# 96 very short matmuls on zeros ahead of the warming matmuls of a chunked-attention and attention-experts kernel

## The chip, the cores and the metric

The kernel runs on one core of one Trainium2 chip. The metric is the device time of one execution in microseconds (us); the medians below are over several executions. A core has five engines that run side by side, each with its own list of instructions, which it takes in order: PE (TensorE, the matrix unit), DVE (VectorE), ACT (ScalarE), POOL (GpSimd) and SP (SyncE, which here only starts DMA transfers). They wait for each other by semaphores. A matmul on PE is two instructions: a weight load (LDWEIGHTS, the rows named PEld) and the matmul proper (MATMUL, the rows named PE).

## The reference

Two stages, all in float32. Batch B = 8, heads 8, sequence S = 576, head width 64.

```python
# stage 1: attention inside chunks of 64 rows, for every head
q_c = q.reshape(B, H, nc, 64, D)            # k_c, v_c alike
scores = scale * np.matmul(q_c, k_c.transpose(0, 1, 2, 4, 3))
attn = softmax(scores)
x = np.matmul(attn, v_c)                    # heads put side by side: x is (8, 576, 512)

# stage 2: four attention experts on x, each token takes two of them
logits = x @ w_gate                         # (8, 576, 4), the two largest per token win
for e in range(4):
    q, k, v = x @ wq[e], x @ wk[e], x @ wv[e]            # width 64
    a = softmax(causal(scale * (q @ k.transpose(0, 2, 1))))
    out += gate[e] * (a @ v @ wo[e])
```

## The kernel before

**Stage 1** goes by groups of 128 rows (36 of them, one or two to a unit). For a group SP loads keys, queries and values (`ks`, `qs`, `vs`, 256 KB each; lines 358, 359 and 362; four buffers of each kind). PE makes the scores as 32 small 64x64 matmuls per group (line 471), which go to the four corners of the array in turn; DVE, ACT and POOL do the softmax (lines 481 to 499); the weights are turned, for the first five groups by PE (line 369, called from line 504) and otherwise by a DMA transpose; and PE makes `x` as 32 matmuls per group (line 544).

**Stage 2** goes by the eight batches: queries and keys of the experts (line 588, three passes of a split into a high and a low part), values and gate logits (line 443), scores of two experts at a time (line 685), exponentials (line 708), turning by PE (line 369), the product with the values (line 779) and the projection out (line 807). The weights `wqk`, `wvg` and `wo` are loaded in the first microseconds (line 412) and split by ACT, DVE and POOL (lines 415 and 419).

**The order.** Every step is added to a plan (`add`, line 75) with its engine, an estimated length and what it depends on. At the end `plan.emit` (line 92) runs through the plan on a clock of its own, with orders that are written out by hand for each engine (`ORDER`, line 191), and emits the instructions in that order. For PE it also fills holes: where PE's next step isn't ready on the planner's clock and the time is before `WARM` (25 us), it emits a **warming matmul** (line 841): 128x512 on the tile `warm`, which is all zeros, into the bank that is last in the list of free banks. The line that does so:

```python
if eng == "PE" and now < until:
    fill()
    free_at[eng] = now + pe_time(0.215, 1.0, now)
```

The planner's clock for PE starts at 0.9 us and is moved only by what `emit` itself emits. 47 warming matmuls come out: 11 ahead of the first real matmuls of line 471, the others between the steps of the first 20 us. `warm` is a 128x512 bf16 tile that DVE zeroes at the start (line 319); `banks` are the eight banks of the accumulator memory. `ctx.enter_context(tc.manual_schedule())` (line 840) makes the framework keep the order in which instructions are issued from there on.

Of the kernel before, what the change touches and what calls it, by code (L numbers as in the profile page):

```python
# [281 lines left out]
def chunked_attention_then_attention_experts(ctx: ExitStack, tc: tile.TileContext, qt, kt, vt, wqk, wvg, wo, out):  # L282
    nc = tc.nc
    pe, dve, act, pool = nc.tensor, nc.vector, nc.scalar, nc.gpsimd
# [6 lines left out]
    def tiles(n, shape, name, dt=F32, src=None):  # L291
        return [(src or sb).tile(shape, dt, name=f"{name}{i}") for i in range(n)]

    banks = tiles(8, [128, 512], "bank", src=psum)
# [23 lines left out]
    warm = sb.tile([128, 512], BF16, name="warm")  # L318
# [477 lines left out]
    def project_out(b):  # L796
        bb = b // 2
        y_op[b] = []
        for t in (range(4) if b % 2 == 0 else range(4, 9)):
            bk, y = Slot(banks), Slot(y_p)  # L800

            def f(t=t, bk=bk):
                w = [t_.rearrange("p (k c) -> p k c", k=2) for t_ in W["wo"]]
                n = 0
                for k in range(2):
                    for up, wp in ((uh, w[0]), (ul, w[0]), (uh, w[1])):
                        pe.matmul(bk.t, up[:, k, 128 * t:128 * t + 128], wp[:, k, :], start=(n == 0), stop=(n == 5))  # L807
                        n += 1
            o = add("PE", 1.41, f, deps=u_op[b] + (u_op[b - 1] if t == 4 else []) + w_op["wo"], uses=[bk])
            y_op[b].append(o)  # L810
            if t % 2:
                o = add("ACT", act_t(512), lambda bk=bk, y=y: act.activation(y.t, bk.t, AF.Copy), deps=[o],
                        uses=[bk, y])
            else:
                o = add("DVE", dve_t(512), lambda bk=bk, y=y: dve.tensor_copy(y.t, bk.t), deps=[o], uses=[bk, y])

            def f(t=t, y=y):
                nc.sync.dma_start(out[bb * 2 * S + 128 * t:bb * 2 * S + 128 * t + 128], y.t)
            o = add("SP", 0.36, f, deps=[o], uses=[y])
            transfer("store", 0.6, o, [y])  # L820
# [6 lines left out]
    for b in range(B):  # L827
# [10 lines left out]
            values(b, pair)  # L838
        project_out(b)
    ctx.enter_context(tc.manual_schedule())  # L840
    plan.emit(lambda: banks and pe.matmul(banks[-1], warm[:, 0:128], warm, start=True, stop=True), WARM)  # L841


# [37 lines left out]
```

## Time and profile before

| | |
|---|---|
| Median of 3 executions | 382.74 us (382.62 to 382.85) |
| The profiled execution | 382.36 us |
| Its span, from the first to the last instruction | 380.4 us |
| PE, matmuls | 372.2 us busy, 5213 instructions |
| PE, weight loads | 315.7 us busy, 5215 instructions |
| ACT / DVE / POOL | 302.6 / 268.5 / 245.1 us busy |
| Mean granted clock of TensorE | 1.000 |
| Warming matmuls (line 841) | 13.2 us busy |
| Instruction transfers, queue q8 | 41 packets, 0.67 MB |

How to read the lines. A row of a **timeline** has the start in us from the span's start, the length, the engine, the line of the kernel, the operation, output and inputs by the program's names, the shape, the number of instructions merged into the row, and in brackets the idle time before it with what ended it. The **chain of waits** follows the work that ended last back to its cause; its rows have start, length and work. A row of **windows** has the stretch, its length, then for each engine the busy time and, in brackets, how many instructions lie in the stretch, then the granted clock, the DMA engines' busy share and GB/s; the columns are PE, PEld, DVE, ACT and POOL, or PE and PEld alone. "issue" means that the engine waited for nothing that the profile shows. Matmuls are pipelined and their ends are modelled: the distance between starts is the safer measure. An "x" ahead of a number is a count. Instructions that only wait are not in the counts.

### The profile page before, as it was taken

The numbers are of one execution on the slowest core, as the hardware profiler recorded it, in microseconds if no ns is written. First come the engines' busy times: TensorE is split into PE (matmuls) and PEld (weight loads), VectorE is DVE, ScalarE is ACT, GpSimd is POOL, SyncE is SP. The second block draws the span as 40 slices with busy tenths as digits, with TensorE's granted clock in tenths as the row PEclk, the third lists the DMA queues.
The fourth block names the chain that finished last, engine by engine and source line by source line (L and its number), as shares of the span: only waits on it lengthen the run. The fifth ranks groups of instructions, "written<-read, shape, count | busy, mean of one in ns | idle before, by whom it ended". The sixth has DMA issues, their size and how long they took to land.

```text
span 380.4 us, 13426 instructions
## 1 busy us (share of the span) xinstructions
PE 372.2 (98%) x5213; PEld 315.7 (83%) x5215; DVE 268.5 (71%) x895; ACT 302.6 (80%) x844; POOL 245.1 (64%) x447
## 2 busy tenths in 40 slices
PE   8999999999999999999999999998999999999996
PEld 3598999977888899788779999877898899977664
DVE  3668878589898775668978487597994298467442
ACT  3555699999958998799887579988996579899731
POOL 7552678986885469975864448959387048876600
PEclk9999999999999999999999999999999999999999
DMA  8977785527779493276989473446786101236534
GB/s 269 392 258 236 201 177 169 98 71 146 130 228 246 93 221 83 57 134 91 293 220 271 137 180 72 112 65 214 142 197 87 25 30 30 30 57 84 165 140 165
DMA packets 88479, 57.24 MB, mean 150 GB/s; under 512 B 68960, under 2 KB 68960, under 8 KB 88416
## 3 DMA queue, kind: packets, MB, share of 16 engines
q1 hardware_dynamic: 88272, 56.12, 59.7%
q8 instruction: 41, 0.67, 0.7%
q10 hardware_dynamic: 144, 0.26, 0.3%
q14 instruction: 22, 0.18, 0.2%
HBM read 30.42 MB, written 9.44 MB: 105 GB/s over the span
## 4 chain that ended last, share of the span: by engine, by line
PE 80%; ACT 9%; DVE 3%; POOL 2%; issue 2%; DMA 2%; POOLq 0%; ACTq 0%; DVEq 0%
PE bank L588 22%; PE bank L443 12%; PE bank L807 12%; PE bank L779 9%; PE bank L685 9%; PE bank L544 4%; PE bank L471 4%; PE bank L369 4%; PE bank L841 3%; ACT at L708 3%; DMA wpT<-wp 2%; POOL at L730 1%; ACT aT L754 1%; ACT aT L385 1%; DVE at L696 1%
## 5 line engine op out<-in xcount | busy, mean ns | idle before, releaser
L730 POOL TENSOR_SCALAR at<-at,st,gate 128x448 f32<-128x448 f32 (+4 forms) x160 | 94.9, 607 | 25.1 <-DVE st L721 21.8
L708 ACT ACTIVATE at<-at,st 64x64 f32<-64x64 f32 (+4 forms) x160 | 88.8, 565 | 4.3 <-DVE st L696 4.1
L588 PE MATMUL bank<-xh,wqk_hi 128*128 128x288 f32 x256 | 77.3, 302 | 0.1
L588 PE MATMUL bank<-xl,wqk_hi 128*128 128x288 f32 x256 | 75.4, 295 | 0.0
L588 PE MATMUL bank<-xh,wqk_lo 128*128 128x288 f32 x256 | 75.4, 294 | 0.0
L696 DVE CUSTOM_DVE_ANT_0 at<-bank,mask 128x448 f32<-128x448 f32 (+4 forms) x160 | 59.9, 421 | 8.0 <-PE bank L685 5.7
L499 POOL TENSOR_TENSOR en<-e,mx 128x512 f32<-128x512 f32 x36 | 37.6, 1058 | 38.3 <-DVE mx L490 23.0
L588 PEld LDWEIGHTS bank<-xh,wqk_hi 128*128 128x128 f32 x256 | 48.0, 187 | 2.5 <-issue 1.0
L588 PEld LDWEIGHTS bank<-xl,wqk_hi 128*128 128x128 f32 x256 | 48.0, 188 | 0.5 <-issue 0.3
L588 PEld LDWEIGHTS bank<-xh,wqk_lo 128*128 128x128 f32 x256 | 48.0, 188 | 0.0
L779 PE MATMUL bank<-aT,vv 128*64 128x448 f32 (+4 forms) x384 | 47.0, 393 | 0.4 <-ACT aT L385 0.3
L779 PEld LDWEIGHTS bank<-aT,vv 128*64 128x64 f32 x384 | 25.0, 137 | 22.3 <-issue 13.7
L385 ACT ACTIVATE aT<-wpT 128x1024 uint16<-128x1024 uint16 x32 | 37.7, 1187 | 3.3 <-DMA wpT<-wp 3.2
L754 ACT ACTIVATE aT<-bank 128x128 f32<-128x128 f32 (+1 forms) x160 | 37.2, 331 | 3.3 <-PE bank L369 2.9
L385 ACT ACTIVATE et<-wpT 128x1024 uint16<-128x1024 uint16 x31 | 36.5, 1183 | 3.6 <-DMA wpT<-wp 3.4
L762 DVE STREAM_TRANSPOSE aT<-at 32x96 f32<-32x96 f32 x128 | 34.4, 269 | 5.3 <-PE bank L779 2.4
L443 PE MATMUL bank<-wvg_hi,xh 128*128 128x260 f32 x128 | 37.0, 289 | 0.0
L376 POOL COPY wp<-at 128x1024 uint16<-128x1024 uint16 x32 | 32.5, 1033 | 6.3 <-DMA wpT<-wp 6.1
L443 PE MATMUL bank<-wvg_lo,xh 128*128 128x260 f32 x128 | 36.3, 283 | 0.0
L443 PE MATMUL bank<-wvg_hi,xl 128*128 128x260 f32 x128 | 36.0, 281 | 0.0
L685 PE MATMUL bank<-kh,qh 64*128 64x288 f32 (+4 forms) x192 | 32.3, 326 | 0.6 <-ACT qh L596 0.5
L376 POOL COPY wp<-en 128x1024 uint16<-128x1024 uint16 x31 | 31.6, 1039 | 1.4 <-DMA wpT<-wp 1.1
(104 smaller groups left out, 895.6 us busy)
## 6 DMA issues: line engine op xcount, KB each, us to landing
ks<-in_kt_dram SPq DMA_DIRECT2D x36, 256.0 KB, 4.4
vs<-in_vt_dram SPq DMA_DIRECT2D x36, 256.0 KB, 4.4
out_dram<-y SPq DMA_DIRECT2D x36, 256.0 KB, 2.1
qs<-in_qt_dram SPq DMA_DIRECT2D x35, 256.0 KB, 4.7
at<-in_wqk_dram SPq DMA_DIRECT2D x4, 256.0 KB, 5.5
wpT<-wp SPq DMA_TRANSPOSE x63, 3.8
at<-in_wvg_dram SPq DMA_DIRECT2D x2, 260.0 KB, 5.6
at<-in_wo_dram SPq DMA_DIRECT2D x2, 256.0 KB, 5.9
```

The costliest lines, as they stand in the source:

```text
L376: pool.tensor_copy(p.t[:, :256 * n].rearrange("p (x n) -> p x n", x=2), src().bitcast(U16).rearrange("p (n x) -> p x n", x=2))
L385: act.activation(put().bitcast(U16).rearrange("p j (q x) -> p j q x", x=2), pt.t[:, :256 * n].rearrange("p (x j q) -> p j q x", x=2, j=n), ...
L443: pe.matmul(bk.t[0:rows, :W_VG], xp[:, k, cols], wp[:, k, :], start=(n == 0), stop=(n == 3 * KT - 1))
L499: pool.tensor_tensor(en.t.rearrange("p (s h k) -> p s h k", s=2, h=HP), ev, rv.to_broadcast([128, 2, HP, 64]), op=OP.mult)
L588: pe.matmul(bk.t[:, :288], wp[:, k], xp[:, k, c0:c0 + 288], start=(n == 0), stop=(n == 3 * KT - 1))
L685: pe.matmul(bks[s].t[:rows(i), at:at + c1 - c0], q[own, cs], k[own, c0:c1], start=(x == 0), stop=(x == 2), skip_group_check=True)
L696: dve.tensor_tensor_reduce(out=a.t[:r, A_OFF[i] + c0:A_OFF[i] + c1], in0=bk.t[:r, at:at + w], in1=mask[:r, m0:m0 + w], scale=1.0, scalar=f ...
L708: act.activation(af, af, AF.Exp, scale=-1.0, bias=st.t[:r, 0, i, 0:1], accum_out=st.t[:r, 1, i, 0:1])
L730: pool.tensor_scalar(af, af, st.t[:r, 2, i, 0:1], gt.t[:r, i, e:e + 1], op0=OP.mult, op1=OP.mult)
L754: act.activation(dst, bk.t[:, s0:s0 + 64 * n].rearrange("p (j c) -> p j c", j=n), AF.Copy)
L779: pe.matmul(bk.t[64 * s:64 * s + 64, c0 - h0:h1 - h0], vs.t[:, j, 64 * (2 * pair + s):64 * (2 * pair + s) + 64], ts[s].t[:, 448 * j + c0:4 ...
L807: pe.matmul(bk.t, up[:, k, 128 * t:128 * t + 128], wp[:, k, :], start=(n == 0), stop=(n == 5))
```

## The change

Right before the planner emits anything, 96 matmuls are issued on PE. Each loads 64 columns of the zero tile as weights and streams 16 columns of it, into the first 64 partitions and 16 columns of the last bank. That is 96 weight loads and 96 matmuls, 192 instructions, at the front of PE's list. They read what the warming matmuls read, and write where those write. Nothing else is changed: the plan, its clock and the warming matmuls stay as they are.

```diff
     ctx.enter_context(tc.manual_schedule())
+    for _ in range(96):
+        pe.matmul(banks[-1][0:64, 0:16], warm[:, 0:64], warm[:, 0:16], start=True, stop=True)
     plan.emit(lambda: banks and pe.matmul(banks[-1], warm[:, 0:128], warm, start=True, stop=True), WARM)
```

## The prediction

> **What bounds the kernel now.** I read the head of the page first: the span, the engines' busy shares and the chain that ended last.
>
> ```profile
> span 380.4 us, 13426 instructions
> ...
> PE 372.2 (98%) x5213; PEld 315.7 (83%) x5215; DVE 268.5 (71%) x895; ACT 302.6 (80%) x844; POOL 245.1 (64%) x447
> ...
> PE 80%; ACT 9%; DVE 3%; POOL 2%; issue 2%; DMA 2%; POOLq 0%; ACTq 0%; DVEq 0%
> ```
>
> PE is busy for all but 8.2 us, and it carries four fifths of the chain. A busy matmul row is not a matmul at its peak, so I asked next what PE waits for, in the view of waits for PE alone. These are all its rows (us in total, times, longest):
>
> ```profile
> PE bank L544 <- issue: 1.3, 1, 1.3
> PE bank L841 <- DVE warm L319: 1.2, 1, 1.2
> PE bank L471 <- issue: 0.6, 1, 0.6
> PE bank L685 <- ACT qh L596: 0.5, 1, 0.5
> PE bank L841 <- issue: 0.3, 2, 0.2
> PE bank L779 <- ACT aT L385: 0.3, 1, 0.3
> ```
>
> Only 0.5 + 0.3 us of this is a wait for another engine in mid-kernel. PE takes its instructions in order, so what is put in front of them moves nearly everything behind, to the end: about 0.8 us at most can be swallowed on the way. What counts is by how much the head grows, and what the shift does to the two long "issue" waits. The head, in PE's timeline (start, length, then the work), with one row of SP's timeline and one of the page's DMA issues:
>
> ```profile
> 1.24 4.87 PE L841 MATMUL bank<-warm 128*128 128x512 bf16 x11 [1.24 <-DVE warm L319]
> 6.05 0.69 PE L471 MATMUL bank<-ks,qs 64*64 64x64 f32 x32
> 6.67 0.61 PE L841 MATMUL bank<-warm 128*128 128x512 bf16 x2
> 7.32 0.69 PE L471 MATMUL bank<-ks,qs 64*64 64x64 f32 x32
> 8.17 4.05 PE L841 MATMUL bank<-warm 128*128 128x512 bf16 x18 [0.16 <-issue]
> ```
>
> ```profile
> 1.25 0.91 SPq L358 DMA_DIRECT2D ks<-in_kt_dram  x2
> ```
>
> ```profile
> ks<-in_kt_dram SPq DMA_DIRECT2D x36, 256.0 KB, 4.4
> ```
>
> The first keys are asked for at 1.25 and land, by the page's median, 4.4 us later, at about 5.7; the first real matmuls (L471) start at 6.05. So the 11 warming matmuls ahead of them cover a real wait almost exactly, and some 0.4 us is left under that cover: nothing hides further work put before them. The planner's clock doesn't know of the new matmuls, so it emits all the warming ones as before.
>
> The rows also show the array's rate. 11 warming matmuls take 4.87 us, 18 later ones 4.05: 0.44 us against 0.225. The rate doubles once, near 6.1, after 4.8 us of uninterrupted work. The granted clock in the windows further down reads 1.00 from the start, so this factor isn't read from there.
>
> **First term: 96 tiny matmuls.** Each loads a 128x64 weight and streams 16 columns, at the half rate. No such pair is in the trace. Nearest are the 128x64 loads at the end of an L779 group, each with a 64-column matmul (a window of L779 alone); then the transposes of L369, with 128-column loads (a piece of the chain); then the 64x64 pairs of L471 above, which go to four corners of the array in turn.
>
> ```profile
> 356.63:356.75 0.12, 0.12 (x8) 0.11 (x4) 1.00 0.00 0
> ```
>
> ```profile
> 153.75 1.03 PE bank L369 x28
> ```
>
> The window's PEld count says that 4 loads begin in 0.115 us: 29 ns a pair. L369 gives 37, and L471 (6.67 - 6.05) / 32 = 19. I take the first, which has the same weight shape, doubled for the half rate: 57 ns, 96 x 57 = 5.5 us. The ends are 19 ns, if the tiny pairs are bound by issue alone (1.9 us), and twice 37, if their loads take as long as the transposes' (7.1 us).
>
> Then the warming ones. A warming matmul streams columns all the time, a tiny one 14 ns (16/512 of 440) of its 57. I credit the tiny stretch with that quarter of its 5.5 us, 1.3 us, towards the 4.8 that the doubling needed. The remaining 3.5 us are 8 warming matmuls at 0.44, and the last 3 at 0.225 take 0.7: 4.2 us, where 6.05 - 1.24 = 4.8 were needed before. The head grows by 5.5 + 4.2 - 4.8 = 4.9 us. With no credit it would be 5.5, with full credit 2.9 (first rival).
>
> The Trainium skill ("TensorE: Matmul & The Clock Gate", Part 1, "What's actually happening") has the rate decided in free-running windows of some 3.4 us, so that the next edge after 6.1 would be near 9.5. By that rule the head would grow by 4.5 us. The trace shows one switch only and can't tell this from my count.
>
> Of this, 0.2 comes back. The two warming matmuls from 6.67 need 0.45 and the second L471 starts only at 7.32, held by its data; later these will have landed. The loads that SP holds until PE frees a buffer move along with PE, and whoever waits for L471 (DVE first) moves too; I add nothing for them, since the wait only shifts. Head: +4.7 us.
>
> **Second term: the stalls inside a group.** The two "issue" waits lie inside runs of identical matmuls, where no data is waited for (PE's timeline, and one group of 64 from the chain):
>
> ```profile
> 32.95 1.09 PE L471 MATMUL bank<-ks,qs 64*64 64x64 f32 x58
> 34.65 0.34 PE L471 MATMUL bank<-ks,qs 64*64 64x64 f32 x6 [0.61 <-issue]
> 34.92 0.40 PE L588 MATMUL bank<-xh,wqk_hi 128*128 128x288 f32 x1
> ...
> 262.42 1.46 PE L544 MATMUL bank<-et,vs 64*64 64x64 f32 x87
> 265.19 0.38 PE L544 MATMUL bank<-et,vs 64*64 64x64 f32 x9 [1.31 <-issue]
> 265.50 0.81 PE L779 MATMUL bank<-aT,vv 128*64 128x128 f32 x6
> ```
>
> ```profile
> 41.58 1.09 PE bank L471 x64
> ```
>
> A group of 64 takes 1.09 us, 17 ns each; the first stalled one took 34.92 - 32.95 = 1.97, so 0.9 was lost. The second run needed 96 x 17 ns = 1.6 and took 3.1: 1.5 lost. What is missing there? PE's code comes in pieces, by the page's queue table, and counting PE and PEld between the stalls tells where pieces end:
>
> ```profile
> q8 instruction: 41, 0.67, 0.7%
> ```
>
> ```profile
> 0.00:34.60 34.60, 32.44 (x599) 22.70 (x601) 20.46 (x51) 18.04 (x43) 18.29 (x49) 1.00 0.81 287
> 34.60:111.92 77.32, 77.12 (x1266) 68.04 (x1267) 63.43 (x216) 68.00 (x191) 61.45 (x105) 1.00 0.65 157
> 111.92:265.10 153.18, 151.28 (x2162) 132.76 (x2160) 114.28 (x385) 131.16 (x360) 104.73 (x187) 1.00 0.68 156
> ```
>
> PE and PEld have 10,428 instructions for 41 pieces: 254 to a piece (PE's own wait instructions, which the views leave out, come on top). Between the stalls lie 2533 + 4322 = 6855 instructions, 27 times 253.9. It is a whole number of pieces, so both stalls sit at a piece's end: where a piece is run through faster than the next can be fetched, PE stands still. With 192 more instructions in front, every end falls 192 instructions earlier in the old order, into other work. In the next fence stand the two old pieces that end in a stall, one as short that doesn't, and then the three shortest pieces of the new cutting, found by counting back (the next has 4.4 us):
>
> ```profile
> 31.09:33.82 2.73, 2.73 (x129) 2.57 (x128) 2.13 (x4) 2.51 (x9) 0.00 (x0) 1.00 0.36 102
> 261.79:263.66 1.87, 1.87 (x142) 1.87 (x135) 1.87 (x10) 1.74 (x7) 1.87 (x3) 1.00 0.42 153
> 197.59:199.88 2.29, 2.29 (x129) 2.19 (x129) 2.29 (x5) 1.78 (x4) 0.00 (x0) 1.00 0.92 287
> 129.74:131.92 2.18, 2.18 (x131) 2.09 (x129) 0.55 (x3) 2.18 (x6) 0.00 (x0) 1.00 0.03 8
> 178.42:180.69 2.27, 2.27 (x129) 2.20 (x132) 1.47 (x9) 2.16 (x7) 1.14 (x2) 1.00 0.95 190
> 219.61:222.16 2.55, 2.55 (x128) 2.39 (x130) 1.43 (x5) 1.16 (x5) 1.72 (x4) 1.00 0.02 5
> ```
>
> The stalled pieces lasted 2.73 + 0.9 and 1.87 + 1.5, so the next piece is there some 3.5 us after one is entered. The piece at 197.59 lasted 2.29 and nothing stalled: it is entered inside an L779 group, whose matmuls are long, so issue had run ahead and asked early. The new one at 129.74 is entered inside an L779 group too, the other two behind L443 and inside L588, which are also slow. Bounds for the new stalls: 0, and 3.5 less each of the three lengths, 3.5 us in sum. By the piece at 197.59, I take 0.2. Second term: -2.4 + 0.2 = -2.2 us.
>
> The Trainium skill ("Runtime: NRT & Kernel Launch", "Instruction fetch mechanics") calls the cost of crossing such a boundary mostly hidden. That holds for 39 crossings here, not for these two; by the rule alone this term would be nought.
>
> **Sum.** +4.7 - 2.2 = +2.5 us. The profiled execution took 382.36 us, its span 380.4 with 2.0 around it; the sum gives 384.9. The median of the runs shown is 382.74, 0.38 higher: 385.2 us. Between 54 and 62 ns a pair, and with half the credit to one and a half times it, the same sum runs from 384.6 to 386.0.
>
> **Rivals.**
> 1. *The tiny matmuls warm the array as well as the others do.* Then the rate doubles near 6.1 as before: 85 tiny pairs at 57 ns, 11 at 29, and all 11 warming ones at 0.225. The first L471 starts at 8.9, +2.9; sum 2.9 - 0.2 - 2.2 = +0.5, 383.2 us. For it: PE is never idle. Against: for three quarters of the time no column streams. Chance 0.20.
> 2. *Faster: the pairs are bound by issue alone*, 19 ns as in L471. 1.9 us, and 4.2 for the warming ones: +1.3; sum 1.3 - 0.2 - 2.2 = -1.1, 381.6 us. It decides below some 30 ns a pair, where the head grows by less than the stalls give back. For it: L471 shows that issue can go so fast. Against: L471 uses four corners in turn, and these all use the same half of the array. Chance 0.13.
> 3. *Slower: so short a matmul doesn't hide the next load*, 74 ns, 7.1 us: +6.5 - 0.2 - 2.2 = +4.1, 386.8 us. Chance 0.17.
> 4. *The stalls stay, or only move* (the upper bound above): +4.7 or more, 387.4 us. For it: 39 of 41 crossings show no stall, so these two might have another cause that stays. Against: the whole number of pieces between them. The Trainium skill's rule on fetch, above, comes to the same time. Chance 0.08.
>
> **How the numbers follow.** The forecast has 0.42. A measurement of this kernel can tell about 0.2%, 0.77 us, from no change. Below -0.77 lies rival 2, at its cheaper prices: 0.12. Within it lie rival 1 and a little of the rest: 0.22. The remainder, 0.66, is slower. The range leaves out rival 2 at the bottom and the worst of rival 4 at the top: 382.2 to 387.5.
>
> **What would show it.** In the changed profile: the tiny stretch's length over 96 (57 ns?); how many of the first 11 warming matmuls start 0.44 us apart (8?); the first L471 near 10.9 instead of 6.05; no "issue" wait inside an L471 or L544 group; and, where one stands, its count from the start. The prediction is wrong if the head grows by under 2.4 us, or if the two stalls are still there.

## The result and the profile after

The changed kernel takes 385.58 us (median; 384.49 to 386.21) where the kernel before, on the same chip, took 382.68 us (382.34 to 382.85): 1.0074 times as long, 95% interval 1.0048 to 1.0099. It is slower by 2.9 us, and 385.2 was forecast. The profiled execution took 384.49 us, the lowest of them.

The head of its page, with the row of the instruction queue (packets, MB, share):

```profile
span 382.5 us, 13617 instructions
...
PE 375.9 (98%) x5308; PEld 319.8 (84%) x5311; DVE 268.3 (70%) x895; ACT 302.6 (79%) x844; POOL 244.9 (64%) x447
...
q8 instruction: 42, 0.69, 0.7%
```

The span grew by 2.1 us and PE's busy time by 3.7: PE works longer and waits less. The instruction queue moved 42 packets instead of 41. What PE waits for now, in the view of waits for PE (all its rows):

```profile
PE bank L842 <- DVE warm L319: 1.2, 1, 1.2
PE bank L843 <- issue: 0.7, 3, 0.3
PE bank L779 <- ACT aT L385: 0.3, 1, 0.3
PE bank L588 <- DVE xl L559: 0.3, 1, 0.3
PE bank L685 <- ACT qh L596: 0.2, 1, 0.2
```

L842 are the tiny matmuls and L843 the warming ones. The two "issue" waits of L471 and L544 are gone; those of L843 are most likely matmuls that the trace misses and no idle time: it has 5308 matmuls to 5311 loads, three fewer, and there are three such waits. L588 has a wait for DVE that it did not have. The places themselves, in PE's timeline:

```profile
1.24 5.29 PE L842 MATMUL bank<-warm 128*64 128x16 bf16 x96 [1.24 <-DVE warm L319]
6.87 3.91 PE L843 MATMUL bank<-warm 128*128 128x512 bf16 x10 [0.33 <-issue]
10.71 0.69 PE L471 MATMUL bank<-ks,qs 64*64 64x64 f32 x32
...
11.87 0.69 PE L471 MATMUL bank<-ks,qs 64*64 64x64 f32 x32
...
37.50 1.11 PE L471 MATMUL bank<-ks,qs 64*64 64x64 f32 x64
38.55 0.40 PE L588 MATMUL bank<-xh,wqk_hi 128*128 128x288 f32 x1
39.22 0.40 PE L588 MATMUL bank<-xl,wqk_hi 128*128 128x288 f32 x1 [0.27 <-DVE xl L559]
...
266.13 1.58 PE L544 MATMUL bank<-et,vs 64*64 64x64 f32 x96
267.65 2.92 PE L779 MATMUL bank<-aT,vv 128*64 128x128 f32 x24
```

The kernel before, for one start that the prediction did not show:

```profile
35.16 0.29 PE L588 MATMUL bank<-xl,wqk_hi 128*128 128x288 f32 x1
```

Take the start of each matmul after, less its start before. That curve says where the time came from:

| matmul | before | after | shift |
|---|---|---|---|
| first L471 | 6.05 | 10.71 | +4.66 |
| L471 ahead of the first stall | 32.95 | 37.50 | +4.55 |
| first L588 behind it | 34.92 | 38.55 | +3.63 |
| second L588, on `xl` | 35.16 | 39.22 | +4.06 |
| L544 ahead of the second stall | 262.42 | 266.13 | +3.71 |
| L779 behind it | 265.50 | 267.65 | +2.15 |

The head adds 4.66 us, the first stall's end gives back 0.92, and the second's 1.56. Between them 0.43 of the first gain is lost again at once: the second L588 needs `xl`, which DVE has only just made. DVE was now later than PE, where the stall had hidden it. Ahead of the second stall a further 0.35 is gone. The old wait of L685 for `qh` has shrunk from 0.5 to 0.2 us; a short gap inside L588 that the kernel before had at 112.3 (shown with the run of 256 pairs) gives back 0.3; and other short shifts lose about as much. Beyond the second stall nothing more happens, and the span is 2.1 us longer.

### The profile page after: what moved, and what is told of

Same layout as the page of the kernel before. It is cut to its first block, busy times and chain, and to the rows that moved or that the text cites. A ratio compares the mean times of both kernels' runs of the same rounds, so it can differ in the third digit from the quotient of the medians.

```text
span 382.5 us, 13617 instructions
## 1 busy us (share of the span) xinstructions
PE 375.9 (98%) x5308; PEld 319.8 (84%) x5311; DVE 268.3 (70%) x895; ACT 302.6 (79%) x844; POOL 244.9 (64%) x447
## 4 chain that ended last, share of the span: by engine, by line
PE 76%; DVE 8%; ACT 5%; POOL 4%; DMA 3%; issue 3%; POOLq 0%; ACTq 0%; DVEq 0%
PE bank L588 24%; PE bank L443 12%; PE bank L807 9%; PE bank L685 9%; PE bank L779 8%; PE bank L544 4%; DMA wpT<-wp 3%; PE bank L369 3%; PE bank L843 3%; PE bank L471 3%; DVE at L696 2%; POOL at L730 2%; ACT at L708 1%; DVE aT L762 1%; PE bank L842 1%
## 5 line engine op out<-in xcount | busy, mean ns | idle before, releaser
L588 PE MATMUL bank<-xh,wqk_hi 128*128 128x288 f32 x256 | 77.3, 302 | 0.1
L588 PE MATMUL bank<-xl,wqk_hi 128*128 128x288 f32 x256 | 75.5, 295 | 0.3 <-DVE xl L559 0.3
L588 PE MATMUL bank<-xh,wqk_lo 128*128 128x288 f32 x256 | 75.4, 294 | 0.0
L588 PEld LDWEIGHTS bank<-xh,wqk_hi 128*128 128x128 f32 x256 | 48.0, 188 | 2.5 <-issue 1.0
L588 PEld LDWEIGHTS bank<-xl,wqk_hi 128*128 128x128 f32 x256 | 48.0, 188 | 0.7 <-DVE xl L559 0.5
L588 PEld LDWEIGHTS bank<-xh,wqk_lo 128*128 128x128 f32 x256 | 48.0, 188 | 0.0
L779 PE MATMUL bank<-aT,vv 128*64 128x448 f32 (+4 forms) x384 | 46.7, 393 | 0.4 <-ACT aT L385 0.3
L779 PEld LDWEIGHTS bank<-aT,vv 128*64 128x64 f32 x384 | 24.1, 137 | 22.9 <-issue 14.5
L481 DVE TENSOR_REDUCE mx<-bank 128x8 f32<-128x512 f32 (+1 forms) x44 | 24.0, 581 | 13.4 <-PE bank L471 13.3
```

Of the source, the lines that this page charges most:

```text
L588: pe.matmul(bk.t[:, :288], wp[:, k], xp[:, k, c0:c0 + 288], start=(n == 0), stop=(n == 3 * KT - 1))
L779: pe.matmul(bk.t[64 * s:64 * s + 64, c0 - h0:h1 - h0], vs.t[:, j, 64 * (2 * pair + s):64 * (2 * pair + s) + 64], ts[s].t[:, 448 * j + c0:4 ...
```

## The experiments

The prediction's theory is that the 96 pairs cost a fixed time at the front, and that the two stalls are ends of pieces of PE's code, so that they depend on the count of instructions ahead of them and on nothing else. The rival is that the stalls went because everything behind the head now runs later, beside other DMA traffic. The expectations give the theory that I held by then as A and its rival as B. All kernels compute the whole reference. Each change is shown against the changed kernel; ratios are against the kernel before, with their 95% intervals.

### The pairs, the count and the delay

**The changed kernel unaltered**, to see how its head varies.

> The changed kernel once more, unaltered, for the spread of its times. Theory A (the moment at which the array's rate doubles differs from run to run and falls on the warming matmuls): times spread over some 1.7 us as in the first four runs (384.5 to 386.2), and the profiled run's span follows its doubling: 10.1 us gave a first L471 at 10.7 and 382.5 us of span; a doubling later by x lengthens the span by about x/2, and a run never comes out below about 384.3. Theory B (chance differences in mid-kernel): a like spread, but with the same head in the profile, and the difference somewhere later. No long issue wait inside an L471 or L544 group under both.

385.25 us (384.43 to 386.51), ratio 1.0071 (1.0048 to 1.0093). Its head, in PE's timeline:

```profile
6.46 4.84 PE L843 MATMUL bank<-warm 128*128 128x512 bf16 x11
11.24 0.69 PE L471 MATMUL bank<-ks,qs 64*64 64x64 f32 x32
```

With no record missing, the tiny stretch is seen to last from 1.24 to 6.46: 54 ns a pair. But here all 11 warming matmuls take 0.44 us, where 8 of 11 did in the profile above (10.71 - 6.87 = 3.84 us for ten is 7 or 8 at 0.44; the one whose record is missing ran at half rate too, and by the starts in the trace it makes 8 in all). The head grew by 5.19 us, not 4.66. So the array's rate doubles at another time in each execution. The 385.71 us of this profile are 1.2 above the other one; 0.5 of that is the head. Where the rest arises, short waits of L588 and L369 of 0.3 and 0.2 us stand which the other profile lacks; I did not pursue them.

**128 pairs instead of 96**: 256 instructions in front, which is one whole piece.

```diff
-    for _ in range(96):
+    for _ in range(128):
```

> 128 tiny pairs in place of 96: 256 instructions, a whole piece. Theory A (the stalls sit where pieces of code end, so only the count matters): both stalls are back at the very same matmuls of L471 and L544, 0.8 and 1.5 us. The head grows by 32 x 53 ns = 1.7 us more than with 96, some 6.4 over the kernel before; in all +6.2, about 389 us. Theory B (any delay of PE gets the stalls out of the way): no stall, +6.4 - 0.2 - 2.4 = +3.8, about 386.5 us.

388.71 us (388.13 to 390.21), ratio 1.0167 (1.0140 to 1.0193). PE's timeline:

```profile
8.16 4.68 PE L843 MATMUL bank<-warm 128*128 128x512 bf16 x11
...
39.56 1.09 PE L471 MATMUL bank<-ks,qs 64*64 64x64 f32 x58
41.19 0.34 PE L471 MATMUL bank<-ks,qs 64*64 64x64 f32 x6 [0.53 <-issue]
...
269.98 1.46 PE L544 MATMUL bank<-et,vs 64*64 64x64 f32 x87
273.00 0.38 PE L544 MATMUL bank<-et,vs 64*64 64x64 f32 x9 [1.57 <-issue]
```

Both stalls are back, and at the very same matmuls: 58 and 6, 87 and 9, as in the kernel before, although all of it runs 6.6 to 7.6 us later. A delay alone does not remove them; 64 instructions more undo what 192 did. The tiny stretch grew by 8.16 - 6.46 = 1.70 us for 32 pairs, 53 ns each.

**20 more warming matmuls in place of the 96**: about the same delay, but only 40 instructions.

```diff
-    for _ in range(96):
-        pe.matmul(banks[-1][0:64, 0:16], warm[:, 0:64], warm[:, 0:16], start=True, stop=True)
+    for _ in range(20):
+        pe.matmul(banks[-1], warm[:, 0:128], warm, start=True, stop=True)
```

> 20 more of the ordinary warming matmuls (128x512) in place of the 96 tiny pairs: nearly the same delay of the head, but 40 instructions only. They run at the doubled rate: 20 x 0.215 = +4.3 us at the head. Theory A (count): the piece ends move by 40 instructions and stay in dense work; by the cutting counted from the trace before some 3 us of stalls remain, in other groups of L471 and L544; +4.3 - 0.2 + 0.7 = +4.8, about 387.5 us. Theory B (delay): no stall, +4.3 - 0.2 - 2.4 = +1.7, about 384.4 us.

387.4 us (385.96 to 388.02), ratio 1.0114 (1.0084 to 1.0144). PE's timeline:

```profile
116.82 0.34 PE L471 MATMUL bank<-ks,qs 64*64 64x64 f32 x7 [1.22 <-issue]
...
268.26 1.21 PE L544 MATMUL bank<-et,vs 64*64 64x64 f32 x67
270.53 0.69 PE L544 MATMUL bank<-et,vs 64*64 64x64 f32 x29 [1.06 <-issue]
```

The head grew by 3.7 us (first L471 at 9.78). The delay theory said 384.4 and falls. The second stall now comes after 67 pairs of L544 instead of 87: 20 pairs, exactly the 40 instructions, earlier. The first one has left its group, and one of 1.2 us appears at 116.8, in a run of L471 where no other profile above has one: moving the ends can also make a stall. The waits of PE have a third, of 0.2 us in L544 at 205.4.

**Four corners**: the same count, with 64x64 weights that go to the four corners of the array in turn, as in L471.

```diff
-    for _ in range(96):
-        pe.matmul(banks[-1][0:64, 0:16], warm[:, 0:64], warm[:, 0:16], start=True, stop=True)
+    for n in range(96):
+        r, c = 64 * (n % 2), 64 * (n // 2 % 2)
+        pe.matmul(banks[-1 - n % 2][c:c + 64, 0:16], warm[r:r + 64, 0:64], warm[r:r + 64, 0:16], start=True, stop=True)
```

> The same 96 pairs and 192 instructions, but 64x64 weights on 64 rows, sent to the four corners of the array in turn, as L471 does. Theory A (a tiny pair's price is the load of its 64 columns at the half rate, 53 ns, and four corners load side by side): 53 / 4 = 13 to 19 ns a pair, 1.3 to 1.9 us; the stalls are gone as with the changed kernel; +1.7 - 0.2 - 2.4 = -0.9, about 381.8 us. Theory B (each pair costs 53 ns whatever its corner, an issue price): 5.1 us and 385.5 us as the changed kernel.

382.38 us (380.94 to 383.15), ratio 0.9989 (0.9974 to 1.0004). PE's timeline:

```profile
1.24 1.46 PE L843 MATMUL bank<-warm 64*64 64x16 bf16 x96 [1.24 <-DVE warm L319]
2.63 4.88 PE L844 MATMUL bank<-warm 128*128 128x512 bf16 x11
7.44 0.69 PE L471 MATMUL bank<-ks,qs 64*64 64x64 f32 x32
```

(2.63 - 1.24) / 96 = 14.5 ns a pair. The head grows by 1.39 us, no stall of L471 or L544 is left, and the profiled span is 379.3 us, 1.1 under that of before. This is the second rival's outcome: a head that grows by less than the stalls give back. Whether issue alone bounds these pairs, as it had it, or four loads side by side (a quarter of 53 ns is 13), this run doesn't tell. The profiled execution, at 381.35 us, is one of the shorter ones. The median gains nothing that can be told from no change; the executions spread over 2.2 us.

### What the tiny pairs do for the array's rate

**256 pairs**, 13.7 us of them.

```diff
-    for _ in range(96):
+    for _ in range(256):
```

> 256 tiny pairs: 512 instructions, two whole pieces, so the stalls are back at the same L471 and L544 matmuls (0.8 and 1.5 us). Theory A (a stretch of tiny pairs doesn't count as work for the doubling of the rate): all 256 keep 53 ns, 13.65 us, the rate doubles only 3.4 us or more after the first warming matmul, and the whole is +13.3, about 395.7 us. Theory B (they count, for a quarter of their time, as the prediction had it): 256 x 53 ns hold enough of it; the rate doubles within the tiny stretch or at the latest 1.5 us after it, and the whole is 1 to 6 us shorter than under A.

396.84 us (395.6 to 398.26), ratio 1.0382 (1.0356 to 1.0408). Two windows with the tiny pairs alone (busy time and, in brackets, the instructions in the stretch, for PE and PEld; then the granted clock, the DMA engines' share and GB/s), then PE's timeline of the head:

```profile
2.00:4.00 2.00, 2.00 (x41) 2.00 (x41) 1.00 0.82 215
12.00:14.00 2.00, 2.00 (x41) 2.00 (x40) 1.00 1.08 394
```

```profile
1.24 13.82 PE L842 MATMUL bank<-warm 128*64 128x16 bf16 x256 [1.24 <-DVE warm L319]
15.40 3.55 PE L843 MATMUL bank<-warm 128*128 128x512 bf16 x10 [0.33 <-issue]
```

41 pairs in the first stretch and 41 in the last: in 13.7 us of them the rate does not double. This refutes the first rival, that they warm the array as the others do. Of the eleven warming matmuls behind them (the record of one is missing) about seven still run at half rate: in the trace the rate doubles at 17.88, 2.9 us after the first of them. Neither theory has that: B, with the credit of a quarter, allowed 1.5 us at most, A 3.4 at least. So the credit fails, but whether the pairs count for nothing or for a smaller part this run doesn't tell. The granted clock in the windows reads 1.00 in both, so it does not show this state.

The waits of PE:

```profile
PE bank L544 <- issue: 1.3, 1, 1.3
...
PE bank L588 <- issue: 0.4, 1, 0.4
```

The stall of L544 came back, and one of 0.4 us stands in L588. 512 instructions are two whole pieces, so all the ends should fall at the same matmuls as before. They do, in smaller sizes too: the L471 group, first below, takes 1.41 us where it took 1.11 without a stall, with the longest gap after 58 matmuls again; and the kernel before has a short gap at the very matmul of L588, in the other two rows:

```profile
45.68 1.41 PE L471 MATMUL bank<-ks,qs 64*64 64x64 f32 x64
```

```profile
112.00 0.30 PE L588 MATMUL bank<-xh,wqk_hi 128*128 128x288 f32 x1
112.32 0.40 PE L588 MATMUL bank<-xl,wqk_hi 128*128 128x288 f32 x1
```

The two starts lie 0.32 us apart where 0.13 is usual in L588. The stall at 116.8 of the run with 20 warming matmuls is this crossing as well: counted from the end of PE's list, it comes 20 pairs ahead of it.

What decides the size can be read from the traces, which hold every packet of the instruction queue. In the kernel before, one landed at 33.26 and PE went on at 34.65; another landed at 263.84 and PE went on at 265.19. They are the 4th and the 31st, 27 pieces apart, as the prediction had counted. In all the traces together PE has 13 "issue" waits inside L471, L544, L588 and L779, and each ends 1.3 to 1.6 us after such a packet landed. So the stalls are waits for code, and a crossing costs the time by which PE comes too early for it.

**32 columns instead of 64.**

```diff
-        pe.matmul(banks[-1][0:64, 0:16], warm[:, 0:64], warm[:, 0:16], start=True, stop=True)
+        pe.matmul(banks[-1][0:32, 0:16], warm[:, 0:32], warm[:, 0:16], start=True, stop=True)
```

> The same 96 pairs and 192 instructions with 32 instead of 64 weight columns. Theory A (the price is the load, so many columns at the half rate): 27 ns a pair, 2.6 us; head +2.5, stalls gone, 0.4 given back to the new wait at 35: +2.5 - 0.2 - 2.4 + 0.4 = +0.3, about 382.7 us. Theory B (a fixed price per pair on one place of the array): 53 ns, and 385.3 us as the changed kernel.

382.22 us (381.28 to 384.61; one execution of 712.28 us, whose cause I don't know, is left out of the spread and of the ratio), ratio 1.0006 (0.9988 to 1.0024). PE's timeline:

```profile
1.24 2.73 PE L842 MATMUL bank<-warm 128*32 128x16 bf16 x96 [1.24 <-DVE warm L319]
```

The stretch takes 2.73 us where 64 columns took 5.29: half the columns loaded, half the time, with the same 16 streamed. The first L471 starts at 7.54 instead of 6.05, 1.5 us later and not 2.5 as expected, because here the rate doubles 2.4 us after the first warming matmul. The stalls are gone as with 64. The same 192 instructions thus cost 2.9 us in one form and nothing that can be measured in another.

### Looking for a version that beats both

The corners form with some warming matmuls left out keeps the count at 192 more (196 in the first version) and should give the head's growth back. The first two versions each have a twin without the pairs, which is the kernel before with the same `fill`. The first leaves out 12 (four of the first 11, eight of the 19 ahead of the third L471), with 110 corner pairs (the loop of the corners run with `range(110)`, not shown again):

```diff
+    calls = []
+    def fill():
+        calls.append(0)
+        if 7 <= len(calls) - 1 < 11 or 13 <= len(calls) - 1 < 21:
+            return
+        pe.matmul(banks[-1], warm[:, 0:128], warm, start=True, stop=True)
-    plan.emit(lambda: banks and pe.matmul(banks[-1], warm[:, 0:128], warm, start=True, stop=True), WARM)
+    plan.emit(lambda: banks and fill(), WARM)
```

> 110 pairs in the four corners, and 12 of the warming matmuls left out (4 of the first 11, 8 of the later 18): 220 - 24 = 196 instructions more. Theory A (the shift of the cutting is worth 2.4 us wherever it comes from, the head is filler that can be taken out down to the data): first L471 near 6, the third near 11.3 where it was 12.15, both stalls gone: -0.9 - 2.4 + 0.4 = -2.9, about 379.5 us. Theory B (the head can't be shortened, since what follows it waits for data anyway): -2.0, about 380.4 us.

385.41 us (385.31 to 385.78), ratio 1.0086 (1.0073 to 1.0099): slower than before, which neither theory had. PE's timeline, then three windows (PE, PEld, DVE, ACT, POOL, then the granted clock):

```profile
8.31 0.69 PE L471 MATMUL bank<-ks,qs 64*64 64x64 f32 x32 [0.55 <-DMA qs<-in_qt_dram]
10.21 4.22 PE L850 MATMUL bank<-warm 128*128 128x512 bf16 x10 [1.20 <-DVE e L483]
```

```profile
10.00:12.00 2.00, 1.74 (x5) 0.72 (x6) 1.90 (x6) 1.18 (x3) 1.46 (x2) 0.66 1.05 389
12.00:14.00 2.00, 2.00 (x6) 0.64 (x5) 0.83 (x2) 0.64 (x1) 1.73 (x2) 0.50 1.06 387
14.00:16.00 2.00, 2.00 (x39) 1.06 (x38) 0.88 (x3) 0.00 (x0) 1.29 (x2) 0.98 1.05 387
```

PE now waits where it had been filled, 0.55 and 1.20 us within 2.5 us. Then the array falls back to half rate: ten warming matmuls take 4.22 us. The clock column does show this: at 0.50 for half rate, 0.66 and 0.98 make (1 - 0.66) x 2 / 0.5 = 1.4 and 0.1 us around the full 2.0, so 3.4 us at half rate. A stall of 1.0 us in L588 comes on top. The saving is gone. All four executions have a mean granted clock of 0.991 to 0.995, so the fall is in each of them.

**The twin, 12 left out and no pairs:**

> The kernel before with the same 12 warming matmuls left out and no tiny ones: 24 instructions fewer, which moves the piece ends by 24 the other way. Theory A (count): the first stall is gone, one of some 1.7 us stays near the L471 and L544 groups at 262; the head is shorter by 0.9 to 1.6: in all -1.5 to -2.2, about 380.5 us, and the run with the corners is a further 1 us below. Theory B (the filler was needed to keep the rate up): the head's matmuls run at the half rate for longer and the time is 382.4 us or more.

383.35 us (381.62 to 385.93), ratio 1.0038 (1.0014 to 1.0063): with 24 instructions fewer it is slower than before. The profiled execution, at 381.91 us, is one of the shortest, and what made others take up to 385.93 us it does not show. It has the 1.7 us wait for the first keys that the four warming matmuls had covered, and this in PE's timeline:

```profile
263.05 0.43 PE L779 MATMUL bank<-aT,vv 128*64 128x128 f32 x3
264.53 1.83 PE L779 MATMUL bank<-aT,vv 128*64 128x128 f32 x9 [1.04 <-issue]
```

The second stall moved from 87 pairs into L544 to 96 pairs and 3 of the next group: 12 pairs later, the 24 instructions again. Gaps of 1.7 and 1.2 us, longer than in the run before, were followed by no fall of the clock here.

**101 corner pairs, and the five warming matmuls around the third L471 left out** (the condition in `fill` is `31 <= len(calls) - 1 < 36`):

> 101 pairs in the four corners, and the 5 warming matmuls between the third L471 group and the first L369 left out, where PE's next real step has been ready for 2 us: 202 - 10 = 192 instructions more, and PE is not idle longer than about 0.1 us anywhere. Theory A (the price of the front is filler time, and filler that covers no wait can be taken out one for one): 1.1 us below the corners alone, about 381.2 us, 1.0 below the kernel before. Theory B (the removed filler comes back as a wait at the first L369 or L544): within 0.3 us of the corners alone, about 382.4 us.

381.32 us (380.46 to 382.35) against 382.18, ratio 0.9977 (0.9962 to 0.9993). It is the one version of the five whose interval lies below 1, narrowly: the gain is 0.2%. It beats the changed kernel by far more. PE's timeline:

```profile
1.24 1.55 PE L843 MATMUL bank<-warm 64*64 64x16 bf16 x101 [1.24 <-DVE warm L319]
...
15.71 1.65 PE L850 MATMUL bank<-warm 128*128 128x512 bf16 x6 [0.53 <-DVE e L483]
...
263.50 1.58 PE L544 MATMUL bank<-et,vs 64*64 64x64 f32 x96
```

No stall, 1.5 us of pairs, some 1.1 us of filler less, and 0.53 of that back as a wait.

**Its twin, the five left out and no pairs:**

> The kernel before without those same 5 warming matmuls and without tiny ones: 10 instructions fewer. Theory A (count): the piece ends move by 10 the other way and stay in the same dense groups, both stalls stay at about their size (0.7 to 0.8 and 1.4 to 1.7 us); -1.1 from the filler alone, about 381.2 us. Beside the corners run it tells whether the shift of the cutting, bought for 1.4 us at the front, is worth more than it costs: equal times say that it is not. Theory B: the filler comes back as a wait, 382.2 us.

381.88 us (381.28 to 384.05), ratio 0.9987 (0.9970 to 1.0003). PE's timeline:

```profile
32.80 1.44 PE L471 MATMUL bank<-ks,qs 64*64 64x64 f32 x64
...
261.53 1.57 PE L544 MATMUL bank<-et,vs 64*64 64x64 f32 x92
264.52 0.33 PE L544 MATMUL bank<-et,vs 64*64 64x64 f32 x4 [1.42 <-issue]
```

The second stall is where 10 instructions fewer put it, 5 pairs later (92 instead of 87). The first, which theory A kept at 0.7 to 0.8 us, is down to 0.3: its group takes 1.44 us instead of 1.11, and in the trace the gap comes after 63 matmuls, again 5 later. The two intervals of this pair of kernels overlap, so how much of the gain is the pairs' and how much the left-out filler's stays open.

**107 corner pairs and eleven left out** (`31 <= len(calls) - 1 < 42`):

> 107 pairs in the four corners, and the 6 warming matmuls behind the first L369 left out as well as the 5 before it: 214 - 22 = 192 instructions more. In the run with 5 left out those 6 began only after a wait of 0.53 us for DVE, on an accumulator bank that the planner thought free. Theory A (that wait belongs to the filler, and the first L544 is ready about 1 us after the first L369): L544 starts some 1 us earlier, the whole some 0.9 us below the run with 5 left out, about 380.4 us. Theory B (L544's input takes as long as the filler did): 381.3 us, no change against the run with 5 left out.

383.22 us (380.52 to 385.03), ratio 1.0015 (0.9992 to 1.0039). I had expected a gain. The waits of PE:

```profile
PE bank L850 <- ACT et L508: 1.6, 1, 1.6
...
PE bank L471 <- DMA qs<-in_qt_dram: 0.7, 1, 0.7
...
PE bank L369 <- POOL en L499: 0.5, 1, 0.5
```

All three stand in the first 17 us: the filler that was left out comes back as waiting. But this profile is of an execution of 381.9 us, which is below the median of the kernel before, 382.39. Ten of the twelve had a mean granted clock of 0.991 to 0.996 and took 382.77 to 385.03 us; the two at 0.998 and 1.000 took 380.52 and 381.9. So what costs the median its gain is most likely a fall to half rate like that of the first drop experiment, which this profile doesn't have.

**The changed kernel a third time**, for the head:

> The changed kernel a third time, unaltered, for one more head. By the free-running clock windows the rate doubles at some moment 3.4 to 6.8 us after the first warming matmul at 6.4 to 6.5, that is between 9.9 and 13.3, and the first L471 starts between 10.6 and 11.5; by the prediction's credit for the tiny stretch it would start within 0.3 us of 10.9 each time.

385.43 us (384.74 to 386.41), ratio 1.0079 (1.0054 to 1.0103). PE's timeline:

```profile
6.46 4.87 PE L843 MATMUL bank<-warm 128*128 128x512 bf16 x11
11.27 0.78 PE L471 MATMUL bank<-ks,qs 64*64 64x64 f32 x32
```

The head grew by 5.22 us, again with all eleven at half rate. This profile took 385.02 us, 0.5 more than the first one, and the heads differ by 0.56. So the profile that the first section reads is one with a short head, and the 2.1 us of its span understate the 2.8 to 3.0 us of the medians.

## Why the prediction was right

The sum was +2.5 us on the profiled execution; it measured +2.1, and the medians differ by 2.9. Term by term:

| term | forecast, us | measured, us |
|---|---|---|
| price of a pair | 57 ns | 53 to 54 ns |
| head, gross | +4.9 | +4.66, +5.19, +5.22 in three profiles |
| given back at the second L471 | -0.2 | -0.1 |
| the two stalls | -2.4 | -0.92 and -1.56 |
| new stalls in the new cutting | +0.2 | 0 |
| what was late behind the first stall | 0 | +0.43, then -0.35 in all |

**The price** was right, by the row with the same weight shape. The pair costs its loaded columns at the array's rate: 512 streamed columns take 0.44 us, so 64 would take 55 ns, and 32 loaded columns cost half. The second rival's price, below 30 ns, holds for another form, the corners at 14.5 ns, and the third rival's 74 ns for none here.

**The credit** of a quarter was the step that failed. 13.7 us of tiny pairs ran at half rate to the end, and after them the doubling still took 2.9 us of warming matmuls, where the account (4.8 us less a quarter of the 13.7) left 1.4. Nor does it come after a fixed stretch of work: the same kernel had 8 slow warming matmuls once and 11 twice, and over all these traces the doubling came 2.4 us (32 columns) to 5.3 us (five left out, no pairs) after the first warming matmul. That the account's 8 turned up in the first profile is luck. With no credit the prediction's own figure was 5.5, and at the measured price, 96 x 54 ns, it is 5.2: the two longer heads. The rule of the Trainium skill ("TensorE: Matmul & The Clock Gate", Part 1, "What's actually happening") fits the scatter: it says that the same kernel shows a varying number of slow matmuls with the phase of windows that run freely, and its window of some 3.4 us is the 3.4 us of the fall in the first drop experiment. Its sentence that whatever is issued in the first 3.4 us or so runs at the slow rate, and everything after it at the fast one, is not borne out: these pairs ran on at the slow rate for four such stretches. What a window must hold for the rate to rise, and whether tiny pairs count towards it, no run here settles; the two shortest times to the doubling, 2.4 and 2.9 us, both stand behind tiny pairs.

**The stalls** were right in place and size. That they are ends of pieces was only counted in the prediction; the kernels with 256 instructions more (same matmuls), 40 more (20 pairs earlier), 10 fewer (5 later) and 24 fewer (12 later) show it, and so do the packets that land ahead of each stall's end. This refutes the fourth rival. What a crossing costs is not fixed: that of L471 lost 0.9 us in the kernel before and 0.3 with 256 pairs. The rule of the Trainium skill ("Runtime: NRT & Kernel Launch", "Instruction fetch mechanics"), a cost mostly hidden, holds for nearly all the crossings, but in the trace before these two cost 0.9 and 1.5 us.

**What I left out** is what is late next when a stall goes. DVE's `xl` took 0.43 us of the first stall's 0.92; I had looked for new stalls on PE, not for the next producer. Nor had I seen the third crossing, of 0.3 us at L588, which went as well. That these and the wait of L685 nearly cancel is chance.

## What to carry to other kernels

Count the instructions between two unexplained issue waits of one engine: if it is a whole number of pieces, they are most likely waits for code, and every edit ahead of them moves them, for better or worse, whatever else it does. So an edit that adds or removes a few instructions should be judged with that term told apart, for example beside a twin with a whole piece more. And the price of padding is a matter of form: 192 instructions cost 1.4 us in four corners and over 5 us as 64-column loads on one place.

## What the runs showed of the hardware

- Very short matmuls alone do not bring the array's full rate: 256 pairs that stream 16 columns each ran for 13.7 us at 53 ns a pair without a change. The doubling came 2.4 to 5.3 us after the first matmul of 512 columns in these traces.
- The granted clock reads 1.00 at the start although matmuls run at half rate there, but shows a later fall (0.50 for 2 us in the first drop experiment). Gaps of 0.55 and 1.20 us within 2.5 us came ahead of that fall; gaps of 1.7 and 1.2 us in its twin had none behind them, so gaps by themselves do not decide it.
- Pairs in four corners with 16 bf16 columns follow each other at 14.5 ns while the array is at half rate. Those of L471, with 64 f32 columns, slow down with the array: 32 of them take 0.69 us at full rate and 1.13 us at half rate, at 6.05 in the first drop experiment.
- PE goes on 1.3 to 1.6 us after the packet with its next piece of code has landed (13 stalls). With pairs at 17 ns, one such wait cost up to 1.6 us.
